# Transposes as 64x64 tiles, variance by ScalarE squares and output in the score banks, in a fused retention and SoLU kernel

## The chip, the cores and the metric

The kernel runs on one core of a Trainium2 chip. The metric is device time in microseconds (us) of one execution; it is about 1.8 us longer than the span that the profile of the same run shows. PE is TensorE, DVE is VectorE, ACT is ScalarE, POOL is GpSimd. Clock means the TensorE clock that the throttle granted, 1 being full speed.

## The reference

Eight batches of eight heads, 576 positions, head size 64, go through decayed linear attention; its output, 4608 tokens of 512, goes through a layer of 1024 with softmax-weighted units, a layer norm and a second matrix.

```python
def _attn_ref(q, k, v):
    scores = scale * np.matmul(q, k.transpose(0, 1, 3, 2))
    ret = scores * Dmat                      # gamma_h ** (i - j), zero above the diagonal
    return np.matmul(ret, v)

def _moe_ref(x, w_in, w_out, g_ln):
    h = x @ w_in                             # 512 -> 1024
    e = np.exp(h - h_max)
    solu = h * e / (np.sum(e) + 1e-09)
    mu, var = mean(solu), mean((solu - mu) ** 2)
    return ((solu - mu) / np.sqrt(var + 1e-06) * g_ln) @ w_out      # 1024 -> 512
```

## The kernel before

The sequence is cut into windows of 256 positions; 36 attention steps (each a half of the heads of one window) feed 36 token tiles of 128, two tiles to a window. In a step PE makes the transposes of query and key (T), the product with the carried state (I), the masked product (V), the new state (K) and the next scores (S). Then come the first-layer product of a tile (h, "first-layer product t"), exp on ACT, the product with h on DVE (solu), the transposes of solu (L) and the second-layer product (o). The layer norm is folded in: the mean comes in as a rank-one correction (for the first 14 tiles on DVE, later through centered weights w2c), and 1/std, called rstd or rs, as the scale of the last copy.

```python
    CAP = dict(... tp=1, qkT=3, s=1, ... xy=1, ... h=1, e=2, oc=2, solu=3, ... lnT=4, o=1, osb=3)
    # PSUM: tp 1 bank, s 2, xy 2, h 2, o 1: all eight

    def qk_tp(i):                     # 8 transposes of 128x128 into the bank tp
        for n, src in enumerate((d["q16"], d["k16"])):
            for hp in range(2):
                for j in range(2):
                    nc.tensor.transpose(out=tp[:, n, hp, j], in_=src[:, j, 2 * hp : 2 * hp + 2, :], identity=ident)
    def qk_ev(i):
        nc.scalar.copy(out=qkT, in_=tp)                       # ACT
    def stats(t):                     # DVE: two bn_stats and a bn_aggr a tile
        ...
    def mm2(t):                       # second-layer product into its own bank o
        ...
    def o_mean(t):                    # DVE, t < 14, reads PSUM, needs no rstd
        nc.vector.scalar_tensor_tensor(out=d["oc"], in0=nws[:, 0], scalar=mean, in1=d["o"], op0=ALU.mult, op1=ALU.add)
    def o_ev(t):                      # ACT
        nc.scalar.activation(out=d["osb"], in_=d["oc"] if t < NE else d["o"], func=ACT.Copy, scale=rs)
```

The order of the first third is a hand-made list for each engine. Before the first second-layer product, dummy matmuls fill PE's holes, in the bank o.

The softmax here doesn't subtract the row's maximum and nothing guards it: scores larger than these inputs give would overflow.

## Time and profile before

225.67 us, the median of three runs. All times are read off the trace as starts of first-layer products (the first of its eight matmuls); "tail" is from product 35 to the end of the span.

| | product 3 starts | 3 to 16 (13 early steps) | 16 to 31 (15 late steps) | 31 to 35 | tail | span |
|---|---|---|---|---|---|---|
| before | 37.04 | 74.93 (5.76 each) | 79.68 (5.31 each) | 19.00 | 14.92 | 225.6 |

### The profile page before, as it was taken

What the parts mean: (1) busy time and instruction counts of PE and PEld (TensorE: products, weight loads), DVE (VectorE), ACT (ScalarE), POOL (GpSimd) and SP (SyncE); (2) the same over time, 40 slices, a digit from 0 to 9 for tenths busy, and PEclk for the clock granted to TensorE, in tenths of its full rate; (3) what the DMA queues carried; (4) which work ended last, traced back from release to release, by engine and by line L of the source; (5) the groups of instructions that cost most, each with busy time, mean ns of one, the idle gap of its engine ahead of it and who ended that gap; (6) DMA issues with size and microseconds to landing.
All of it is one profiled execution on the core that took longest, in us unless ns stands there. A gap on an engine that the chain in (4) does not pass through costs nothing.

```text
span 225.6 us, 7375 instructions
## 1 busy us (share of the span) xinstructions
PE 208.6 (92%) x2983; PEld 122.0 (54%) x2983; DVE 180.0 (80%) x320; ACT 133.2 (59%) x238; POOL 151.6 (67%) x231
## 2 busy tenths in 40 slices
PE   7876989999699999699999999999999999999991
PEld 2423555656355655465665666666566666555440
DVE  6655798999969898999999877778888888876540
ACT  2454776656457876466666566666665556655641
POOL 3439599999959989929669869695968777311010
PEclk9999999999799999999999999999999999999998
DMA  6999999995594600799987777777764552222334
GB/s 178 351 346 346 326 289 289 293 293 135 132 264 109 191 11 3 179 300 310 294 225 202 236 195 205 202 193 193 209 190 107 145 141 53 49 47 60 84 71 117
DMA packets 65635, 42.64 MB, mean 189 GB/s; under 512 B 4024, under 2 KB 59456, under 8 KB 65600
## 3 DMA queue, kind: packets, MB, share of 16 engines
q1 hardware_dynamic: 65200, 41.96, 67.7%
q8 instruction: 23, 0.38, 0.8%
q10 hardware_dynamic: 400, 0.21, 0.6%
q14 instruction: 12, 0.10, 0.2%
HBM read 32.71 MB, written 9.44 MB: 187 GB/s over the span
## 4 chain that ended last, share of the span: by engine, by line
PE 65%; DVE 17%; DMA 5%; POOL 4%; SPq 4%; issue 2%; ACT 1%; DVEq 0%; POOLq 0%; ACTq 0%
PE h_ps L434 22%; PE o_ps L507 21%; PE xy L314 7%; PE tln L483 5%; PE tqk L291 5%; DVE solu L454 4%; PE s_ps L349 4%; DVE bs L460 3%; DVE ret L382 3%; DMA vr<-in_v_dram 3%; SPq L259 3%; DMA masks<-masks 2%; DVE w L471 2%; DVE oc L515 2%; DVE w L468 1%
## 5 line engine op out<-in xcount | busy, mean ns | idle before, releaser
L434 PE MATMUL h_ps<-w_in,xT 128*128 128x512 f16 x288 | 69.7, 386 | 2.0 <-DVE solu L454 1.9
L454 DVE TENSOR_TENSOR solu<-h_ps,e_sb 128x1024 f16<-128x1024 f32 x36 | 43.9, 1219 | 19.2 <-ACT e_sb L447 19.0
L447 ACT ACTIVATE e_sb<-h_ps 128x1024 f32<-128x1024 f32 x36 | 36.8, 1022 | 31.6 <-PE h_ps L434 31.5
L460 DVE BATCH_NORM_STATS2 bs<-solu 128x6 f32<-128x512 f16 x72 | 46.0, 680 | 0.1
L382 DVE TENSOR_TENSOR ret<-s_ps,masks 128x1024 f16<-128x1024 f32 x36 | 43.8, 1215 | 0.2 <-issue 0.2
L434 PEld LDWEIGHTS <-xT 128*128 128x128 f16 x288 | 27.3, 99 | 30.0 <-issue 4.4
L274 POOL TENSOR_TENSOR k<-kr,small 128x512 f16<-128x512 f32 x36 | 37.5, 1041 | 6.9 <-DMA kr<-in_k_dram 5.1
L507 PEld LDWEIGHTS <-lnT 128*128 128x128 f16 x288 | 25.9, 98 | 27.2
L274 POOL TENSOR_TENSOR q<-qr,small 128x512 f16<-128x512 f32 x34 | 35.2, 1039 | 7.0 <-DMA qr<-in_q_dram 6.9
L507 PE MATMUL o_ps<-w2c,lnT 128*128 128x512 f16 x160 | 38.0, 380 | 0.0
L477 POOL TENSOR_TENSOR rs<-w,small 128x2 f32<-128x2 f32 x18 | 12.4, 691 | 30.0 <-DVE w L471 29.9
L299 ACT COPY qkT<-tqk 128x512 f32<-128x512 f32 x36 | 20.9, 580 | 12.6 <-PE tqk L291 12.6
L416 POOL CAST sbd<-g 64x256 f16<-64x256 f32 x64 | 25.6, 400 | 3.3
L507 PE MATMUL o_ps<-w2g,lnT 128*128 128x512 f16 x112 | 26.5, 379 | 0.0
L422 ACT CAST xT<-xy 128x512 f16<-128x512 f32 x36 | 21.4, 593 | 8.1 <-PE xy L314 6.8
L523 ACT ACTIVATE o_sb<-o_ps,rs 128x512 f32<-128x512 f32 x20 | 13.7, 687 | 20.8 <-PE o_ps L507 12.4
L407 POOL TENSOR_TENSOR g<-tt,small 128x128 f32<-128x128 f32 x32 | 13.4, 418 | 16.4 <-DVE tt L403 16.4
L483 PEld LDWEIGHTS <-solu 128*128 128x128 f16 x288 | 18.6, 98 | 9.3 <-DVE solu L454 2.0
L483 PE MATMUL tln<-ident,solu 128*128 128x128 f16 x288 | 22.1, 220 | 1.0 <-DVE solu L454 1.0
L491 ACT COPY lnT<-tln 128x512 f32<-128x512 f32 x36 | 20.8, 579 | 3.5 <-PE tln L483 3.5
L282 POOL CAST v<-vr 128x512 f16<-128x512 f32 x34 | 20.5, 608 | 1.7 <-DMA vr<-in_v_dram 0.3
L314 PE MATMUL xy<-ret,v 64*64 64x128 f16 x576 | 14.6, 219 | 2.0 <-DVE ret L382 2.0
(51 smaller groups left out, 241.7 us busy)
## 6 DMA issues: line engine op xcount, KB each, us to landing
kr<-in_k_dram SPq DMA_DIRECT2D x32, 256.0 KB, 4.9
vr<-in_v_dram SPq DMA_DIRECT2D x32, 256.0 KB, 5.0
qr<-in_q_dram SPq DMA_DIRECT2D x32, 256.0 KB, 4.8
out_dram<-o_sb SPq DMA_DIRECT2D x64, 128.0 KB, 2.4
w_in_f<-in_moe_w_in_dram SPq DMA_DIRECT2D x4, 512.0 KB, 6.8
w_f<-in_moe_w_out_dram SPq DMA_DIRECT2D x4, 512.0 KB, 7.6
qr<-in_q_dram SPq DMA_DIRECT2D x16, 64.0 KB, 2.2
kr<-in_k_dram SPq DMA_DIRECT2D x16, 64.0 KB, 2.7
```

Of the source, the lines that this page charges most:

```text
L274: eng.tensor_tensor(out=t.rearrange("p j h d -> p h j d"), in0=st[i][nm + "r"], in1=g_of(i, base), op=ALU.mult,)
L299: nc.scalar.copy(out=d["qkT"].rearrange("p n h j q -> p (n h j q)").bitcast(FP), in_=d["tp"].rearrange("p n h j q -> p (n h j q)").bitcast ...
L314: nc.tensor.matmul(start=(c, e) not in begun, stop=False, skip_group_check=True, **kw)
L382: nc.vector.tensor_tensor(out=d["ret"].rearrange("p e h j q -> p (e h) (j q)"), in0=d["s"].rearrange("p e h j q -> p (e h) (j q)"), in1=ma ...
L416: nc.gpsimd.tensor_copy(out=s16[ee[e], :, :, ee[e]], in_=st[i]["g"][ee[e]])
L422: nc.scalar.copy(out=d["xT"].rearrange("p c h q -> p c (h q)"), in_=d["av"][:, :, 0:256])
L434: nc.tensor.matmul(out=h_ps[:, hh], lhsT=st[2 * w + dc // 2]["xT"][:, c, dc % 2], rhs=w_in16[:, dc, hh], start=(dc == 0), stop=(dc == 3),)
L447: nc.scalar.activation(out=d["e"], in_=d["h"], func=ACT.Exp, accum_out=ws[w]["se"][:, c : c + 1])
L454: nc.vector.tensor_tensor(out=d["solu"], in0=d["h"], in1=d["e"], op=ALU.mult)
L460: nc.vector.bn_stats(out=bs[:, half], in_=tk[t]["solu"][:, half * 512 : half * 512 + 512])
L483: nc.tensor.transpose(out=tp[:, c], in_=d["solu"][:, c * P : (c + 1) * P], identity=ident)
L507: nc.tensor.matmul(out=d["o"], lhsT=d["lnT"][:, c], rhs=(w2g16 if t < NE else w2c16)[:, c], start=(c == 0), stop=(c == 7))
```

## The change

Its intent: PE is the busiest engine, so the transposes are made four at a time in the four 64x64 quadrants of the array. Two row halves need two banks, so the output loses its bank and goes into the two score banks. DVE is lightened: the variance becomes a square with a sum on ACT, and in exchange DVE evicts the query and key transposes and centers the weights. All engine orders now come out of a greedy simulation with fixed durations; PE's is a fixed pattern after a given head. The dummy matmuls in the holes are gone, but for the first 12.

```diff
-    CAP = dict(raw=5, qk16=3, v16=4, tp=1, qkT=3, s=1, ... lnT=4, o=1, osb=3)
+    CAP = dict(raw=5, qk16=3, v16=4, tl=1, qkT=4, s=1, ... lnT=6, osb=3)      # tl: 2 banks
+    tl = pools["tl"].tile([P, 2, 2, 512], F16, tag="tl", name="tl")
...
+    for r in range(2):                       # row half r -> bank r, column half c -> partitions
+        for c in range(2):
+            x = 64 * (4 * n + 2 * hp + j)
+            turn(tl[ee[c], r, 0, x : x + 64], d[nm][ee[r], j, 2 * hp + c, :], r)
...
-        nc.scalar.copy(out=d["qkT"]..., in_=d["tp"]...)
+        nc.vector.tensor_copy(out=o, in_=i_)
...
-            nc.vector.bn_stats(...)                                             # and bn_aggr
+        nc.scalar.activation(out=d2, in_=tk[t]["solu"], func=ACT.Square, bias=-mean, accum_out=vs)
...
-            d["o"] = pools["o"].tile([P, DM], FP, tag="o", name="o_ps")
+        x = pools["s"].tile([P, 2, 2, 2, P], FP, tag="s", name="o_ps")
+        d["o"] = x[:, 0].rearrange("p h j q -> p (h j q)")
...
-            out=d["oc"], in0=nws[:, 0], scalar=mean, in1=d["o"], ...            # o_mean, before o_ev
+            out=d["osb"], in0=nws[:, 0], scalar=ws[t // 2]["nr"][...], in1=d["osb"], ...   # after o_ev
...
+        x += [f"T{s + 2}", f"L{s - 4}", f"S{s + 1}", f"M1_{s - 2}", f"M2_{s - 4}"]
...
-                    for _ in range(int((start[o.name] - end_pe - 0.3) / 0.36)):
-                        nc.tensor.matmul(out=wm, lhsT=zeros[:, :P], rhs=zeros, start=True, stop=True)
```

The new fixed pattern (the `x +=` line) puts the second-layer product of a tile (M2) two products of the first layer (M1) after its own.

## The prediction

> **What bounds the kernel now.** I read the busy table and the slices first, then the waits of the middle, then the chain of work that ended last, then the groups of the costliest instructions. The busy table and the slices:
>
> ```profile
> PE 208.6 (92%) x2983; PEld 122.0 (54%) x2983; DVE 180.0 (80%) x320; ACT 133.2 (59%) x238; POOL 151.6 (67%) x231
> PE   7876989999699999699999999999999999999991
> DVE  6655798999969898999999877778888888876540
> POOL 3439599999959989929669869695968777311010
> ```
>
> PE is busiest, but only its right half is solid; on the left it has holes while DVE and POOL stand at 9. The window of the second half:
>
> ```profile
> 109.40:205.40 96.00, 96.00 (x1477) 58.90 (x1467) 79.42 (x145) 58.85 (x111) 64.86 (x104) 1.00 0.62 166
> ```
>
> The columns after the length are busy PE, PEld, DVE, ACT, POOL, clock, DMA. PE is busy 96.00 of 96.00 us and no PE wait appears there, so from 109 to 205 us PE is the bound. The chain of work shows what one step (one token tile) consists of:
>
> ```profile
> 112.14 1.73 PE h_ps L434 x8
> 113.87 0.45 PE tln L483 x8
> 114.31 0.11 PE xy L314 x2
> 114.42 0.35 PE s_ps L349 x16
> 114.77 0.35 PE xy L314 x32
> 115.12 1.83 PE o_ps L507 x8
> 116.95 0.45 PE tqk L291 x8
> 117.40 1.73 PE h_ps L434 x8
> ```
>
> A step is 117.40 - 112.14 = 5.26 us (5.37 where the xy product has four matmuls, 5.31 on average). Transposes are 0.90 of it. Before 109 us the steps are longer: the first-layer products number 3 and 16 start at 37.04 and 111.98 us, 5.76 us a step. There the chain is DVE's:
>
> ```profile
> 47.29 1.13 DVE solu L454
> 48.42 1.13 DVE ret L382
> 49.55 0.66 DVE oc L515
> 50.21 1.21 DVE bs L460 x2
> ```
>
> So three phases matter: a fill (to product 3, 37 us), a DVE-limited stretch of 13 steps, a PE-limited rest; the last product (number 35) starts at 210.65 and the kernel ends 14.95 us after it.
>
> **What the Trainium skill says.** (1) "TensorEngine Tiling (Array Packing)", Key Properties: the four 64x64 tiles work independently, and a change of tiling mode drains the engine. The trace agrees: the 64x64 score matmuls start in groups of four 2 to 4 ns apart, with 56 ns to the next group for 128 columns and 28 to 32 ns for the 64 columns of the state product; where the form changes the gap is about 95 ns longer. (2) "PSUM — Partial Sum Buffer", PSUM bank collisions raise a hardware error: two engines must not use one bank's quadrant at once, reads included. In the trace DVE's state read waits for ACT's copy of another part of the same banks:
>
> ```profile
> 88.59 0.29 DVE L398 TENSOR_TENSOR g<-xy,g 128x128 f32<-128x128 f32 x1 [1.04 <-ACT xT L422]
> 92.06 1.19 DVE L471 TENSOR_TENSOR w<-w,mv 128x2 f32<-128x2 f32 x1
> ```
>
> (3) "SBUF — State Buffer", SBUF: two separate sides: a DVE operation with two SBUF inputs and a GpSimd operation exclude each other. The second line agrees: a 128x2 operation, 0.16 us in its median, took 1.19 us beside a GpSimd operation; its group averages 393 ns. (4) "TensorE: Matmul & The Clock Gate", Part 1: an idle array falls to half clock. The kernel before fills its early holes with 18 dummy matmuls; the first 12, on a cold array, averaged 574 ns, the 18 later ones 383 ns.
>
> **The change part by part.**
>
> Transposes. Per step 8+8 transposes of 128x128 become 32+32 of 64x64: 8 groups of four each. At the state product's 30 ns a group that is 0.25 us in place of 0.45, twice: -0.40 us. The number of form changes stays two per step, as the compiled order has all the 64x64 work in one run. PE step: 5.31 - 0.40 = 4.9 us. If PE stayed the bound, 35 steps would give about -14 us.
>
> Variance. The 72 bn_stats (46.0 us) and 36 aggregates (7.5) leave DVE. ACT gets 36 squares; like its exp (1022 + 194 ns) 1.2 us each, 43.8 us. ACT loses the 36 query/key evictions (20.9) and 8 weight scalings (5.8): 133.2 + 43.8 - 26.7 = 150 us. The build still has one table load, so square and exp share a table.
>
> DVE. It gains the 36 evictions (about 0.6 each from the 512 columns, 22 us), 36 tiny negations (4 us) and 8 weight centerings (0.75 plus port stalls, 8 us); 180 - 53.5 - about 5 of aggregate-linked small work + 34 = about 155 us. The mean correction now adds two SBUF tensors in place of one from PSUM, so it can stall on GpSimd; from the 0.1 to 0.2 us mean excess of the small operations I add 0.2 to its 0.74. No engine but PE is near full.
>
> Output in the score banks. This makes a ring. The scores of a step use the pair of banks, the mask reads them, then the second-layer product writes there, ACT evicts it, then the next scores. Around the ring in the compiled order, with durations of the trace: second product's first matmul to its eviction's start 1.99 (120.31 to 122.30); eviction to ACT's next copy, xT, 0.59; xT to the state read of DVE, which by (2) waits for it, 0.65; state read and its successor 0.54; mask 1.22 + 0.05; then the next second product. Sum 5.03 us. That is longer than PE's 4.9, so it is the ring and not PE that sets the later steps: a gain of 0.28, not 0.40. In the early steps DVE carries mean correction, eviction, product, mask and state: 1.16 + 0.2 + 0.64 + 1.13 + 0.67 + 0.2 + 0.54 + some 0.5 of small ones = 5.0, so the ring or DVE gives 5.1, plus 0.7 for each weight centering.
>
> Fill. The compiled POOL order puts the second state cast behind four loads' work (q2, k2, v2, q3). In the kernel before, q2's work starts at 16.58 us; its q and k scalings take 1.0 and v casts 0.58. So this cast ends at 16.58 + 3 x 1.0 + 0.6 + 0.8 = 21.0, where before the product waiting for it ran at 14.05. First-layer product 0 then starts at about 22.5 instead of 15.28, on a cold array (no dummy matmuls any more), +1.7. The second weight matrix is queued behind step 4's loads: by the positions in the queue and the landings seen before (5.37 MB at 20.5 us, 7.47 MB at 26.25) its last piece lands at 28.4 instead of 26.25. Walking the orders: product 1 at 30.5 (held by DVE's mask, eviction and product), state cast 3 at 35.1, product 2 at 36.6, the weight column sum 38.8 to 40.5, its two ACT copies until 43, only then scores 5 (same banks), mask until 45.5 behind a weight centering, second product 0 until 47.3, product 3 at 48.8. Before: 37.04. The fill loses 11.8 us.
>
> Sum: 48.8 + 11 early steps x 5.12 + 2 without a state product x 4.8 + 4 remaining centerings x 0.7 = 117.5 for product 16 (before 111.98). Fifteen ring steps x 5.05: 193.2. Four shorter last steps, bounded by product-exp-product (4.35 seen at the end before, 4.4 now): 210.9 for product 35. Tail: two second products remain with one output buffer, but the kernel before had four left; by the same durations it comes to 14.9. End: 225.8 us.
>
> **Rivals.** (a) PE stays the bound, the designer's intent: the ring's state read may run before xT in several steps (in the compiled order of some early steps it does), steps of 4.9, and the fill loses only 8 us as loads overlap better. Then 45 + 28 x 4.9 + 17.7 + 14.9 = 215 us. For it: the orders were made by a simulation that aims at 5.0; a change of this size was made to be kept. Against it: in all late steps the state read waits for ACT. (b) Stalls: port stalls of DVE's new two-SBUF-input work, a cold array in the fill, POOL held in turn; 5.3 a step and product 3 at 51 give 51 + 28 x 5.3 + 17.7 + 14.9 = 232. For it: single stalls of over 1 us exist before. Against it: POOL's work falls by the 10.1 us of centering. (c) 64x64 transposes do not run four abreast; then the step stays at 5.3 and the time is that of (b). The state product's groups speak against it. (d) ACT the bound: 4.1 to 4.3 us a step, not likely.
>
> **Range and chances.** The working gives 225.8. I take 224.5, a little to the side of (a), as the list walk sums many waits that may overlap. Rivals (a) and (b) are 215 and 232; I call 217 to 231 the 80% range. Faster by over 2% needs less than 221.2: 0.33. Slower needs more than 230.2: 0.17. Within: 0.50.
>
> **What would show it.** Right if: transposes take 0.25 us per 32; the late steps are 5.0 to 5.1 with PE idle 0.1 to 0.2 a step before the second product, waiting for DVE's mask; product 3 starts at 46 to 51 us; first product 0 after 21 us at half clock; DVE busy about 155, ACT 150. Wrong if: PE has no waits after 60 us and steps of 4.9 (then (a)), if product 3 starts before 44 us, or if the transposes take 0.4 and more.

## More of the kernel before

The two fences here are not in the prediction. The first is PE's clock in 40 slices (tenths of full speed), the second two products of the fill (start, length, engine, line, operation, tiles):

```profile
PEclk9999999999799999999999999999999999999998
```

```profile
23.88 1.89 PE L434 MATMUL h_ps<-w_in,xT 128*128 128x512 f16 x8
...
33.29 1.89 PE L507 MATMUL o_ps<-w2g,lnT 128*128 128x512 f16 x8
```

The clock row stands at 9 from the start, and already first-layer product 1, at 23.88 us, takes 1.89 us (1.82 to the next instruction's start), like second-layer product 0 at 33.29.

Before, for the first 14 tiles, the output's bank came free when the mean correction had read it, which needs no rstd; later it was the ScalarE copy, which does, but no scores stood behind that bank.

## The result, and the profile after

The changed kernel took 242.33 us (237.74 to 242.53, four runs), against 226.32 of the kernel before in the same rounds: slower by a ratio of 1.058 (95% interval 1.043 to 1.073). Ratios are the mean time of one kernel's fast runs over that of the other's of the same rounds, so they are not quite the ratio of the medians. Executions over 1.5% slower than the fastest of the same kernel are left out of the means. Two of six executions counted, and one of these, the profiled one, was the quickest seen. The other four counted as slow only beside it: the control below, the same kernel on another occasion, gave that same level throughout, 241.57 us (240.42 to 242.51), and 1.069. I compare experiments with that control. Both profiles, by the same starts:

| | product 3 | 3 to 16 | 16 to 31 | 31 to 35 | tail | span |
|---|---|---|---|---|---|---|
| predicted | 48.8 | 68.7 | 75.7 | 17.7 | 14.9 | 225.8 |
| changed, first profile | 49.61 | 76.19 | 77.86 | 18.06 | 14.24 | 236.0 |
| changed, control | 52.27 | 76.45 | 78.37 | 18.06 | 14.24 | 239.4 |

Against the kernel before, the control lost 15.2 us in the fill and 1.5 in the early steps, and won 1.3, 0.9 and 0.7 in the three later parts. Against the prediction it is 13.6 us too long: 3.5 in the fill, 7.7 in the early steps, 2.7 in the late ones. The busy table and slices of the first profile:

```profile
PE 199.0 (84%) x4693; PEld 110.9 (47%) x4693; DVE 174.1 (74%) x335; ACT 154.2 (65%) x266; POOL 147.9 (63%) x223
...
PE   7324469499898869898999899999999999999962
...
DVE  6670897978898997899889786868778687663220
...
PEclk9855999799999979999999999999999999999999
```

PE has become less busy, and its left half is no fuller than before. DVE was to fall from 180 to about 155 and stands at 174. The clock row has 8, 5, 5 where it had 9. The waits of the same profile between 50 and 110 us (total us, times, longest):

```profile
ACT o_sb L497 <- POOL rs L477: 8.0, 4, 2.0
...
PE s_ps L343 <- ACT o_sb L497: 5.1, 4, 2.2
```

The output copy waits for rstd, and the next scores wait for that copy. The prediction's ring has the second wait and not the first. Here is one instance in the control, line by line (start, length; DVE, POOL, ACT and PE in turn):

```profile
60.40 0.97 DVE L468 SCALAR_TENSOR_TENSOR w<-se 128x2 f32<-128x2 f32 x1
...
66.28 1.50 DVE L506 SCALAR_TENSOR_TENSOR o_sb<-nws,nr,o_sb 128x512 f32<-128x512 f32 x1
...
60.31 1.03 POOL L255 TENSOR_TENSOR q<-qr,small 128x512 f16<-128x512 f32 x1
...
61.72 0.70 POOL L477 TENSOR_TENSOR rs<-w,small 128x2 f32<-128x2 f32 x1 [0.37 <-DVE w L469]
...
66.19 1.03 POOL L255 TENSOR_TENSOR q<-qr,small 128x512 f16<-128x512 f32 x1
...
62.45 0.69 ACT L497 ACTIVATE o_sb<-o_ps,rs 128x512 f32<-128x512 f32 x1 [2.00 <-POOL rs L477]
...
63.19 0.42 PE L343 MATMUL s_ps<-qkT 64*64 64x128 f16 x16 [0.89 <-ACT o_sb L497]
```

Two things are to be seen. First a chain: DVE's floor of the variance (w, 60.40), GpSimd's power (rs, 61.72), the copy (62.45), the scores (63.19). ACT stood 2 us, PE 0.89. This comes with a window's first tile, because rstd is made for two tiles together and has to wait for the second one: the first six steps are 5.06, 6.21, 5.44, 6.23, 6.06, 7.75. The chain itself has not become slower: in windows 8 to 13 the power ends 8.7 to 8.9 us after the start of the window's second first-layer product, where it took 8.4 to 8.5 in the kernel before. What moved is the copy. From tile 4 to tile 29 the second-layer product started 18.6 to 21.5 us after the first-layer product of its tile; from tile 3 to tile 29 it now starts 11.8 to 17.1 after it. In the kernel before the copy of tile 18 found its rstd 7.25 us old:

```profile
135.62 0.69 POOL L477 TENSOR_TENSOR rs<-w,small 128x2 f32<-128x2 f32 x1 [0.82 <-DVE w L471]
...
143.56 0.69 ACT L523 ACTIVATE o_sb<-o_ps,rs 128x512 f32<-128x512 f32 x1 [1.06 <-issue]
```

In the control the copy of the first tile of each window from 1 to 13 starts 0.03 to 0.06 us after rstd is there. Second, DVE's small instructions are stretched. The floor is 128x2 and took 0.97 us beside a GpSimd scaling that ran from 60.31 to 61.34; the mean correction took 1.50 us beside the next one. The Trainium skill, "SBUF — State Buffer", SBUF: two separate sides, says just this, that a DVE instruction with two SBUF inputs and a GpSimd instruction that reads SBUF hold a port pair in turn for their whole length; the trace agrees. The correction's mean length went from 740 ns (one operand in PSUM) to 1074.

### The profile page after: what moved, and what is told of

Its sections match the earlier page's. It is cut to its first block, busy times and chain, and to the rows that moved or that the text cites.

```text
span 236.0 us, 10927 instructions
## 1 busy us (share of the span) xinstructions
PE 199.0 (84%) x4693; PEld 110.9 (47%) x4693; DVE 174.1 (74%) x335; ACT 154.2 (65%) x266; POOL 147.9 (63%) x223
## 5 line engine op out<-in xcount | busy, mean ns | idle before, releaser
L448 DVE SCALAR_TENSOR_TENSOR solu<-h_ps,e_sb 128x1024 f16<-128x1024 f32 x36 | 44.0, 1221 | 19.1 <-ACT e_sb L441 18.9
L441 ACT ACTIVATE e_sb<-h_ps 128x1024 f32<-128x1024 f32 x36 | 36.9, 1024 | 17.7 <-PE h_ps L428 17.3
L497 ACT ACTIVATE o_sb<-o_ps,rs 128x512 f32<-128x512 f32 x36 | 24.7, 687 | 34.9 <-POOL rs L477 16.5
L460 ACT ACTIVATE d<-solu,nm 128x1024 f16<-128x1024 f16 x36 | 41.5, 1153 | 2.7 <-DVE nm L452 2.4
L490 PE MATMUL o_ps<-w2c,lnT 128*128 128x512 f16 x176 | 41.6, 379 | 1.9 <-ACT lnT L483 1.9
L263 POOL CAST v<-vr 128x512 f16<-128x512 f32 x34 | 23.7, 698 | 3.4 <-PE xy L308 1.9
L298 DVE COPY qkT<-tl 128x512 f32<-128x512 f32 x36 | 24.5, 681 | 0.5 <-PE tl L269 0.3
L343 PE MATMUL s_ps<-qkT 64*64 64x128 f16 x576 | 15.6, 224 | 11.0 <-ACT o_sb L497 7.0
L483 ACT COPY lnT<-tl 128x512 f32<-128x512 f32 x36 | 21.1, 586 | 1.3 <-DVE qkT L298 0.7
L308 PE MATMUL xy<-qkT,sbd 128*128 128x128 f16 (+1 forms) x128 | 12.6, 215 | 10.5 <-POOL sbd L410 9.4
L308 PEld LDWEIGHTS <-sbd 128*128 128x128 f16 x128 | 9.4, 99 | 19.0 <-POOL sbd L410 10.0
```

The costliest lines, as they stand in the source:

```text
L263: copy(out=t, in_=st[i]["vr"])
L298: nc.vector.tensor_copy(out=o, in_=i_)
L308: nc.tensor.matmul(start=(c, e) not in begun, stop=False, skip_group_check=True, **kw)
L441: nc.scalar.activation(out=d["e"], in_=d["h"], func=ACT.Exp, accum_out=ws[w]["se"][:, c : c + 1])
L448: nc.vector.scalar_tensor_tensor(out=d["solu"], in0=d["h"], scalar=1.0, in1=d["e"], op0=ALU.mult, op1=ALU.mult, accum_out=x["ss"][:, c : c ...
L460: nc.scalar.activation(out=d2, in_=tk[t]["solu"], func=ACT.Square, bias=x["nm"][:, c : c + 1], accum_out=x["vs"][:, c : c + 1])
```

## The experiments

Each kernel is the changed one with the edit shown, and was timed in rounds with the kernel before. The first number is the median of all four runs, the second the ratio to the kernel before over fast runs alone; one run of fillwm, warm2 and warm2b and two of bnback counted as slow. "Output right" means that the result passes the comparison. Two give wrong results (norscale and noodrs); one, nood, leaves out a small term and still passes the comparison, but isn't a right kernel either.

### again: the control

> The changed kernel itself, unchanged, as the control of this chip. It should give the same two levels as before: 236 to 238 us with a mean clock near 0.956, and 241 to 242.5 us near 0.93. First-layer product 3 starts near 49.6 us, product 16 near 125.8, product 31 near 203.7 if the profile falls in the faster level. If the profile falls in the slower one, its windows should show in which stage the other 4 to 5 us lie.

241.57 us, ratio 1.0687 (1.061 to 1.077); all four runs between 240.4 and 242.5. The two levels that I expected are not there as such: the first profile's run was the better end. In the control's profile the extra time lies in the fill (product 1 at 30.79 against 29.44, product 2 at 38.72 against 36.03), the later parts are the same to 0.5 us each.

### norscale: the copy needs no rstd

```diff
-        nc.scalar.activation(out=d["osb"], in_=d["o"], func=ACT.Copy, scale=ws[t // 2]["rs"][:, t % 2 : t % 2 + 1])
+        nc.scalar.activation(out=d["osb"], in_=d["o"], func=ACT.Copy, scale=1.0)
```

> The output eviction of ScalarE scales by 1 in place of rstd (a wrong result on purpose), so the score banks come free without waiting for the variance chain (square, floor, GpSimd's power). Theory A, the early steps are long because the eviction waits for rstd: the alternation 5.1/6.2 goes, 13 early steps shrink from 76.2 to 67 to 70 us, the whole by 6 to 9 us. Theory B, the early steps are long because VectorE is full (mean correction, centering, port stalls): under 2 us of gain. Theory C, a cold array in the fill: no gain.

237.61 us, 1.052. The early steps fell only from 76.45 to 73.98 us: the strict pattern of 5.1 and 6.2 went, but steps of 5.1 to 6.8 came in its place. So theory A alone is not the cause; the gain is between the two theories.

### rstile: rstd for each tile

```diff
-            op(f"fl{w}", "DVE", "xx", [f"sp{t - 1}", f"sp{t}"], ...)      # if c: once a window
-            op(f"rs{w}", "POOL", "rs", [f"fl{w}"], ...)
+        op(f"fl{t}", "DVE", "xx", [f"sp{t}"], ...)
+        op(f"rs{t}", "POOL", "rs", [f"fl{t}"], ...)
```

> The floor and rstd are made for each tile in place of each window of two tiles (18 more floor pairs on VectorE, 18 more powers of 0.69 us on GpSimd), result right. An even tile's eviction then needs only its own square, a step earlier. Theory A: the early steps lose most of the waits of the eviction for rstd, 4 to 7 us faster than the changed kernel. Theory B: more VectorE work, so 0 to 3 us slower. Theory C: no change.

238.11 us, 1.052, output right: 3.5 us, just short of theory A. The early steps took 75.78, nearly as before; 1.6 us of the gain is in the late ones (76.76), which now have 5.12 us each. The wait for rstd is gone: from tile 3 on rstd is ready at least 3.0 us before the copy. In the early steps the profile still puts 7.7 us of the copy's waits down to GpSimd (L263), but that is a false name, as here: the instruction named had ended at 66.67 and rstd at 62.99, and the copy starts 0.09 us after the second-layer product ends (65.47 + 1.89 = 67.36):

```profile
65.47 1.89 PE L490 MATMUL o_ps<-w2g,lnT 128*128 128x512 f16 x8
...
67.45 0.69 ACT L497 ACTIVATE o_sb<-o_ps,rs 128x512 f32<-128x512 f32 x1 [0.79 <-POOL v L263]
```

So without the wait for rstd, but with more small work on DVE (70.5 us busy in these steps against 68.9), the early steps gain almost nothing.

### warm: dummy matmuls, placed badly

```diff
+            n = dict(I1=20, S5=4, M2_0=7).get(o.names[0], 0)
+            if n:
+                wm = pools["h"].tile([P, DFF], FP, tag="h", name="wm")
+            for _ in range(n):
+                nc.tensor.matmul(out=wm[:, 0:512], lhsT=zeros[:, :P], rhs=zeros, start=True, stop=True)
```

> Dummy matmuls keep the array busy in the fill: 20 before the second inter-window product (idle 13.3 to 20.8 us), 4 before scores 5 and 7 before the second-layer product 0. Theory C, the cold array and its clock cost time and split the runs in two levels: product 0 takes 1.7 to 1.9 in place of 3.05 us, the second-layer product 0 likewise in place of 3.36, together 2.5 to 3 us, and the slower level of 242 us is no longer seen. Theories A and B: at most 3 us, and the early steps stay at 5.86.

241.11 us, 1.066: no difference from the control. It was no test, though. The dummies write to the first-layer banks, whose former content (the transposed gains) DVE copied out only at 17.9 us. The 20 of them started there and took 6.9 us, 0.35 each; product 0 started at 25.24. The idea is tested again in warm2 below.

### nood: DVE's mean corrections left out

```diff
-        nc.vector.scalar_tensor_tensor(out=d["osb"], in0=nws[:, 0], scalar=nr, in1=d["osb"], op0=ALU.mult, op1=ALU.add)
...
-        nc.vector.tensor_tensor(out=d["nr"], in0=d["nm"], in1=d["rs"], op=ALU.mult)
```

> VectorE's early mean corrections (14 of about 1.07 us) and their scalars (7 of about 0.4 us) are left out, all else in the same order (a wrong result on purpose). Theory B, VectorE is full in the early steps with work that the prediction put at 5.0 us a step and that takes 5.65: removing about 1.3 us a step makes the 13 early steps drop from 76.4 to 66 to 71 us (then the ring or PE sets 5.1 and the waits for rstd stay), the whole by 6 to 10 us against the unchanged kernel's 241.6. Theory A, the wait for rstd sets them: the alternation of 5.1 and 6.2 us stays and the gain is under 3 us.

234.69 us, 1.034. The early steps fell from 76.45 to 70.29, the larger half of what the prediction missed. What is left alternates between 5.13 and 5.6, and in it the copy still waits for rstd. So DVE's load is the larger cause and the wait for rstd the smaller. (In this profile product 3 came at 54.10, 1.8 us later than in the control, as first-layer product 2 ran cold too, 3.43 us; the 70.29 is counted from there.)

### odps: the early output path as before the change

```diff
-            out=d["osb"], in0=nws[:, 0], scalar=ws[t // 2]["nr"][...], in1=d["osb"],
+            out=d["oc"], in0=nws[:, 0], scalar=ws[t // 2]["nm"][...], in1=d["o"],       # before the copy
...
-           lambda t=t: mm2(t), [("s", [f"oe{t}"])], wide=True)
+           lambda t=t: mm2(t), [("s", [f"od{t}" if t < NE else f"oe{t}"])], wide=True)
```

> The early output path as in the kernel before: VectorE corrects the mean straight from the score bank, so only one operand lies in SBUF and no scalar with rstd is needed; ScalarE scales from SBUF later. Result right. Theory B with port stalls: the correction falls from 1.07 to about 0.75 us, the 0.4 us scalars go, and the eviction no longer waits for rstd; early steps 69 to 73 us in place of 76.4, the whole 3 to 7 us faster. If the corrections' place in VectorE's order matters more (the scores now wait for VectorE, which is busy), no gain or up to 3 us of loss.

237.27 us, 1.048, output right. The early steps took 74.23, 2.2 less than the control: short of the range. They became quite regular, eight of thirteen at 5.62 us, and the trace shows why. The correction is now in the score banks' ring and DVE makes it after solu. So solu starts at 113.04, the correction at 114.38, the scores at 115.17 (0.50 us waited for it), the product at 115.52, its exp after it, then the next solu at 118.66: one loop through three engines (DVE, PE, ACT), which no single engine's load shows.

### fillpool: the first state casts ahead of later loads

```diff
-            op(f"sm{i}", "POOL", "st_b", [f"sd{i}"], at(i - 1, 2.2), ...)
+            op(f"sm{i}", "POOL", "st_b", [f"sd{i}"], at(i - 1, 2.2) - (10 if i < 4 else 0), ...)   # and so for sc
```

> In the fill GpSimd makes the first four state products and casts ahead of the query and key scalings of later steps. By the prediction's step on the fill, first-layer product 0 was late because the second state cast stood behind four loads' work: it should start near 15 to 17 us in place of 21.7 to 22.2. If the fill is a chain through that cast, product 3 starts 4 to 6 us earlier than 52 and so does the end; if what comes later (weights, score banks, cold array) sets product 3, it starts within 2 us of where it did.

236.27 us, 1.042, output right. Product 0 started at 16.74, as expected, 5.4 us earlier. Product 3 started only 2.8 us earlier, at 49.51, between the two expectations; the whole gained 5.3 us by the medians. The cast was late as the prediction's walk had it, but half of its lateness was hidden behind what comes after. The first profile of the unchanged kernel also had product 3 at 49.61, so 2 to 3 us here are not much more than the scatter of the fill between profiles.

### fillwm: the weight column sum in the first-layer banks

```diff
-        t = pools["s"].tile(...)[:, 0]...                  # HEAD "... M1_2 T5 WM"
+        t = pools["h"].tile([P, DFF], FP, tag="h", name="w_sum")[:, 0:512]     # after S5
```

> The weight column sum goes to the first-layer banks after scores 5, in place of the score banks before them. By the prediction's step on the fill, scores 5 wait for its two ScalarE copies and second-layer product 0 waits on the mask after them: from product 2 to product 3 takes 13.55 us and should fall to 9 to 11, the end 3 to 4 us earlier. If the second-layer weights' landing sets that stretch, it stays at 13.

243.44 us, 1.069: no gain. From product 2 to product 3 took 14.9 us, not 9 to 11. Scores 5 ran at 41.88 in place of 45.18, but the sum now waited 3.26 us for solu of tile 2, which holds the first-layer banks, and the second-layer product 0 started at 48.95 in place of 47.43. The sum also ran cold (3.60 us in place of 1.90). One bank's wait was traded for another's, so the run neither confirms nor refutes that the score banks set this stretch.

### noodrs: both early suspects away

The edits of nood and norscale together.

> Both suspects of the early steps are taken away at once, in the same order of work: no mean corrections and no scalars for them on VectorE, and the eviction scales by 1, so it waits for no rstd (a wrong result on purpose). So far the first alone gained 6.2 us in the 13 early steps (76.4 to 70.3), the second alone 2.5. If the two together are the whole of what the prediction missed (it had 68.7 us for these steps, with mean corrections), the steps fall to the ring's 5.03 to 5.15 each, 66 to 68 us, with no alternation left. If a third cause holds them, they stay at 70.

231.55 us, 1.024. The early steps took 69.04 us, 7.4 less than the control, a little above the 66 to 68 expected: most steps are 5.0 to 5.1, one is 6.53 (four weight centerings lie near there), a few 5.5. The prediction had 68.7 for these steps. So the wait for rstd and DVE's correction work with its stalls together account for the early miss. But the run takes the corrections away whole (14 us less DVE work in these steps), not only what they cost beyond the prediction. The windows from 60 to 109 us, of the control and of this run (busy PE, PEld, DVE, ACT, POOL, then clock, DMA, GB/s):

```profile
60.00:109.00 49.00, 42.49 (x1046) 24.13 (x1045) 44.29 (x80) 31.97 (x56) 35.12 (x52) 0.97 0.62 165
```

```profile
60.00:109.00 49.00, 46.38 (x1166) 26.50 (x1165) 40.90 (x76) 35.24 (x64) 40.09 (x59) 1.00 0.70 197
```

In the control DVE is the busiest of the five, in this run PE.

### tp128: 128x128 transposes in the changed kernel

```diff
-            turn(tl[ee[c], r, 0, x : x + 64], d[nm][ee[r], j, 2 * hp + c, :], r)     # 32 of 64x64
+            nc.tensor.transpose(out=tl[:, n, 0, x : x + P], in_=d[nm][:, j, 2 * hp : 2 * hp + 2, :], identity=ident)
...                                      # solu's likewise; T and L are 0.45 in the simulation's durations
```

> The transposes of the changed kernel are again of 128x128 (8 and 8 a step, 0.45 us each group, one quadrant at a time), all else kept but the simulated order that follows. My reading of the changed kernel: early steps are not PE's, so they change by under 2 us; the late steps are PE's and the ring's at 5.02 to 5.15 us, and PE's own work goes to 5.3 to 5.4, so the 15 late steps take 79.5 to 82 in place of 78.4 and the last four 19 in place of 18.1: 2 to 5 us slower in all. If the tiles did not run four abreast or did not matter, no change.

249.93 us, 1.105, output right: 8.4 us of the medians slower than the control (1.105 against 1.069), more than the 2 to 5 expected. The early steps stayed (76.98), the late ones took 83.54, 5.57 each in place of 5.22; 2.4 us of the loss lie in the fill (product 3 at 54.62). PE was busy for 83.4 of the 83.54 us. A late step of the control and the same part of tp128:

```profile
173.31 1.89 PE L490 MATMUL o_ps<-w2c,lnT 128*128 128x512 f16 x8
175.03 0.28 PE L308 MATMUL xy<-qkT,sbd 128*128 128x128 f16 x2
...
175.61 0.30 PE L269 MATMUL tl<-ident,q 64*64 64x64 f16 x16
175.74 0.31 PE L269 MATMUL tl<-ident,k 64*64 64x64 f16 x16
175.86 0.49 PE L269 MATMUL tl<-ident,solu 64*64 64x64 f16 x32
176.17 0.41 PE L343 MATMUL s_ps<-qkT 64*64 64x128 f16 x16
```

```profile
163.85 0.40 PE L277 MATMUL tl<-ident,q 128*128 128x128 f16 x4
164.08 0.39 PE L277 MATMUL tl<-ident,k 128*128 128x128 f16 x4
164.30 0.61 PE L282 MATMUL tl<-ident,solu 128*128 128x128 f16 x8
164.84 0.42 PE L339 MATMUL s_ps<-qkT 64*64 64x128 f16 x16
```

Counted from start to start, the transposes take 176.17 - 175.61 = 0.56 us as 64x64 tiles and 164.84 - 163.85 = 0.99 as 128x128; the state product before them, which the larger form has to wait for, gives another 0.1. The step grew from some 5.1 us (where nothing else waits) to 5.57, nearly as much. So in the late steps PE is the bound, and the 64x64 tiles are worth what PE saves there.

### bnback: variance on DVE, query and key evictions on ACT

```diff
-        nc.scalar.activation(out=d2, in_=tk[t]["solu"], func=ACT.Square, bias=..., accum_out=...)
+        for half in range(2):
+            nc.vector.bn_stats(out=bs[:, half], in_=tk[t]["solu"][:, half * 512 : half * 512 + 512])
+        nc.vector.bn_aggr(out=x["mv"][:, c], in_=bs)
...
-        nc.vector.tensor_copy(out=o, in_=i_)        # qk_ev
+        nc.scalar.copy(out=o, in_=i_)
```

> The exchange between VectorE and ScalarE is undone in the changed kernel: variance by VectorE's statistics again (1.3 us and an aggregate a tile), query and key evictions on ScalarE again. VectorE gains about 0.75 us a step. If VectorE is what the early steps wait for, they take 83 to 88 us in place of 76.4; the late steps, where VectorE has 5 us of room in 20, change by under 2 us. Whole: 7 to 13 us slower. If VectorE is not the limit, under 3 us, or even a gain, as the variance is then a ScalarE square and a queue shorter.

253.16 us, 1.110, output right (its two fast runs took 250.67 and 251.43). The early steps took 84.76 us, within the range for a full DVE; but DVE was busy for only 74.7 of them (68.9 of 76.45 in the control), so waits grew with its work. The late ones took 83.74, which I had not expected: they alternate between 5.06 and 5.84, and ACT's copy waits for rstd 16 times in the run, 22.4 us in all. With the variance in DVE's queue rstd comes later, and the score banks wait for it there too. So the exchange of work is worth 4% inside the changed kernel, and the new ring makes a late rstd dear everywhere. The new durations also changed the simulated order of the fill: the second state cast came at 14.07 in place of 20.31 and product 3 at 47.67, which hides 4.6 us of the loss.

### ne4: a right version from these findings

```diff
-NE = 14
+NE = 4                                              # 4 mean corrections; with rstile and fillpool
...
-  op(f"wp{x}", "DVE", "wp", [f"lwo{c}", "gc", "nw1"], at(6 + x * 0.75, 4.0), ...)
+  op(f"wp{x}", "DVE", "wp", [f"lwo{c}", "gc", "nw1"], at(5 + x * 0.4, 2.0), ...)
```

> A right version from what the runs showed: weight centering on VectorE as early as it can be, so that only 4 in place of 14 tiles need a mean correction; floor and rstd for each tile; GpSimd's first four state casts ahead of later loads. If VectorE's corrections and the wait for rstd are the early loss and the state cast a part of the fill's: product 3 at 49 to 51, the 13 early steps 66 to 70, 16 to 31 as in the run with rstd for each tile (76.8), the whole 224 to 230 us, that is 11 to 17 faster than the changed kernel and about level with the kernel before.

232.75 us, 1.029, output right, just above the range. From product 7 on the early steps are 5.0 to 5.5, but the four steps after product 3 took 27.8 us, because the centerings moved there.

### warm2: a warm array in the fill

```diff
-    op("gc", "DVE", "gc", ["G"], at(3, 0.0), ...)
+    op("gc", "DVE", "gc", ["G"], at(-2, 0.0), ...)       # the gains' copy early: it holds the banks
...
+            n = {'S0': 7, 'I0': 4, 'I1': 31, 'S5': 5, 'M2_0': 7}.get(o.names[0], 0)      # and 42 before M1_1
+            for _ in range(n):
+                nc.tensor.matmul(out=..., lhsT=zeros[:, :P], rhs=zeros, start=True, stop=True)
```

> The first warm run was no test: its dummies stood behind a copy of the gains that VectorE made only at 17.9 us, and ran cold. Here that copy is early and dummies fill the holes from the start: 17 before the first transpose, 7, 4 and 31 before scores 0 and the inter-window products 0 and 1, 42 small ones before first-layer product 1, 5 and 7 before scores 5 and second-layer product 0. If the missing dummies (which the change took out) are a part of the fill's loss: the granted clock of the slices up to 50 us is 0.9 to 1, the products of 3.2 to 3.6 us take 1.9, product 3 starts 3 to 6 us before 52, the end likewise, and the run-to-run spread of 236 to 242 us narrows. If VectorE and GpSimd set the fill, product 3 moves by under 1.5 us.

Three runs took 238.0 to 240.6 us at clocks of 0.98 (ratio 1.056); the profiled one took 711.62. It says nothing of the kernel: the matmuls ran at about a quarter of full speed. The group of the first-layer products in this run (busy us, mean ns, idle before; in the control 73.2 and 400):

```profile
L428 PE MATMUL h_ps<-w_in,xT 128*128 128x512 f16 x288 | 239.1, 1077 | 0.0
```

From one product's start to the next operation's start it took 6.3 to 6.6 us for eight matmuls there, some 0.8 each, against 0.22 between most matmuls of the control.

### ne4warm: both together

The edits of ne4 and of warm2, with 11 dummies in place of 31 before inter-window product 1, as that hole is shorter here.

> The right version of before (early centering, 4 corrections, rstd for each tile, early state casts) with the array kept busy in the fill in the same way. If both add up: product 3 at 44 to 47 in place of 49.3, the whole 3 to 5 us under 232.75, 227 to 230, still not under the kernel before. If the fill there is set by VectorE's centering, no gain over 1.5 us.

231.59 us, 1.023, output right. Product 3 came at 44.62, as expected, but the step after it took 9.83 us, and the end moved by only 1.2 us. DVE and PE in that step:

```profile
45.53 1.83 DVE L562 SCALAR_TENSOR_TENSOR w2c<-w_f,gln,nws 128x512 f16<-128x512 f32 x2
...
49.68 2.55 PE L490 MATMUL o_ps<-w2g,lnT 128*128 128x512 f16 x8 [3.16 <-ACT e_sb L441]
```

DVE put two centerings ahead of the state read, which came only at 47.28; ACT's copies and exp stood behind that read, and DVE's mask, which second-layer product 1 must await too, ended at 49.6. The line names the exp; both came last at nearly the same time. What a warm PE saved, DVE's order took back.

### warm2b: the profile that was missing

> The same kernel as warm2 once more, as its profile fell in one run of 710 us (its three other runs took 238.0 to 240.6 at a clock of 0.98). Expected: a median of 238 to 241, the clock row at 9 up to 50 us, the first-layer products 0 and 1 and second-layer product 0 at 1.9 us in place of 3.2 to 3.6. If the cold array is worth its 4 to 5 us of longer products, product 3 starts at 47 to 49; if other engines set the fill, at 50 to 52.

238.66 us, 1.049, output right. Products of the fill in the control and here, then the clock row of this run:

```profile
30.79 3.56 PE L428 MATMUL h_ps<-w_in,xT 128*128 128x512 f16 x8 [2.65 <-DVE solu L448]
...
47.43 3.20 PE L490 MATMUL o_ps<-w2g,lnT 128*128 128x512 f16 x8 [1.83 <-DVE ret L376]
```

```profile
30.57 1.89 PE L428 MATMUL h_ps<-w_in,xT 128*128 128x512 f16 x8
...
36.82 3.38 PE L428 MATMUL h_ps<-w_in,xT 128*128 128x512 f16 x8
...
47.03 1.89 PE L490 MATMUL o_ps<-w2g,lnT 128*128 128x512 f16 x8 [0.21 <-DVE ret L376]
```

```profile
PEclk9999797999999998999999999999999999999999
```

The cold products are back at 1.89 (one, at 36.82, isn't), product 3 starts at 50.24, 2.0 us earlier, and the ratio is 2.0 points lower. What the cold array is worth is not sharp: 2.0 us at product 3, 2.9 by the medians, some 4.5 by the ratio, whose interval (1.037 to 1.061) just touches the control's (1.061 to 1.077); warm2's ratio of 1.056 is 2.8 us. The scatter of the fill is of this size too. So 2 to 4.5 us; at product 3 less than the 4 to 5 of the longer products. Product 3 is at the edge of the second expectation, that other engines set the fill.

### n8warm and n8head: last tries

n8warm has 8 corrections and centerings spread from step 7 on; n8head besides puts product 3 ahead of scores 5, brings the first transposes of solu forward and leaves out the 12 dummies before scores 5 and second-layer product 0. Both have the other edits of ne4warm.

```diff
+NE = 8
+  op(f"wp{x}", "DVE", "wp", [f"lwo{c}", "gc", "nw1"], at(7 + x * 0.5, 0), ...)
+        if s == 4:                                                  # n8head
+            x = "WM I4 V4 K5 T6 M1_3 S5 M2_0".split()
```

> As ne4warm, but with 8 corrections and the weight centering spread over steps 7 to 11, as in ne4warm two centerings ahead of a state read cost the step after product 3 nearly 5 us (9.83 us long). Product 3 at 44 to 45 again, that step 5 to 6.5, the whole 224 to 228, 4 to 7 under ne4warm's 231.6 and about level with the kernel before. If VectorE takes the time back later, under 2 us.

231.24 us, 1.017, output right: no more than ne4warm within the intervals. Product 3 came at 46.06 and the step after it took 7.33, both longer than expected.

> As n8warm, with first-layer product 3 ahead of scores 5 in PE's order, where the array stood idle for two waits. Product 3 at 37 to 40; the end within 1.5 us of n8warm's if the score banks' ring (weight sum, scores 5, second product 0) sets this stretch, 2 to 4 us earlier if PE's own order did.

230.26 us, 1.016 (1.008 to 1.024). Product 3 started at 37.37, as early as in the kernel before, and product 4 at 53.73, where n8warm has 53.40. So PE's order was not what set this stretch. In this trace second-layer product 1 waited 3.54 us, until 47.77, for DVE's mask, which stood behind a floor of 0.90 us, a scalar, a weight centering of 1.16 and the state reads; then it ran cold, 3.57 us. This is the best right version; its ratio lies 1.6% above the kernel before, by less than the 2% at which a verdict is given (it is "unclear", as for noodrs, ne4warm and n8warm). No run beat the kernel before.

## Why the prediction was wrong

It said 224.5 us, 217 to 231, and slower with a chance of 0.17. By its own steps:

**Transposes: right, a little mis-sized.** The query and key transposes took 0.25 us as it said, those of solu 0.31. The two together fell by 0.33 us (0.89 to 0.56), not 0.40. In the late step of 5.02 us, attention's four products took 0.93 us where they had taken 0.81, most of it at the inter-window product (0.21 for 0.11); that gave 0.12 back. The step shortened by 0.24, so PE's own step is 5.02 to 5.1, not 4.9. The ring's terms, by the way, add up to 5.04 and not 5.03.

**"It is the ring and not PE that sets the later steps": the number stood, the mechanism fell.** Late steps free of other waits are 5.08 to 5.12 us on average (15 of them took 76.16 to 76.76 in n8warm, noodrs and rstile) where it said 5.05. But PE has no idle time left there, and tp128 lengthened the step by nearly the whole of what it added to PE. Rival (a), PE as the bound, was right for this part, only at 5.1 and not 4.9; that the ring's 5.05 came so near was luck. The late stretch also had 2 us more of single stalls: one step of 6.23 with a wait for rstd, one of 6.08 in which PE stood 0.84 us for nothing that the profile shows.

**Early steps, "the ring or DVE gives 5.1": this is the step that failed.** Its sum for DVE was right. The instructions of the control's 13 early steps, each counted to the next one's start, add up to about 66 us without the four centerings, 5.1 a step against 5.0. With the centerings DVE was busy for 68.9 us, about the 68.7 that the prediction gave the whole stretch; but the stretch took 76.45 (5.88 a step), as DVE also stood idle for 8.0. The prediction gave it no idle time, though the kernel before had 5.7 us of it there (busy 69.2 of 74.93).

Two things were missing. The ring had no term for rstd. "Second product's first matmul to its eviction's start 1.99" was read at tile 14, whose copy does need rstd, but in an order where rstd had been there for 6.3 us; with the second-layer product moved a step or more forward it was not, and the chain square, floor, power, copy, scores became part of the ring. And the two bounds were joined as a maximum. DVE stands inside the ring (state read, mask, floor), so a full DVE makes rstd and the masks late, and late scores leave DVE idle. The runs size it: 2.5 us for rstd alone (norscale), 6.2 for the corrections alone (nood), 7.4 for both (noodrs), of a miss of 7.7. How much each wait inside the loop takes is not shown: with rstd early by 3 us (rstile) the early steps kept 75.8, so rstd is the smaller part. No run put the second-layer product back by a step, which would test the order itself.

**DVE at 155 us: wrong by 19.** Both kernels' tables give the terms. The corrections grew by 4.6 us in all (10.4 to 15.0, 1.07 each), which the sum had left out. It took off 5 us of small work, but the floor's two instructions cost 11.6 us before and after. It did not list the reads of the accumulators (3.0) and the corrections' scalars (2.7). The evictions took 24.5 in place of 22, the negations 5.5 in place of 4. The stretching by GpSimd, for which 0.2 us was put on a correction, is in some of these: in the control the 13 first instructions of the floor that overlapped GpSimd work averaged 0.59 us, the other five 0.15.

**Fill: right in size, partly in cause.** 48.8 us for product 3, 49.6 and 52.3 measured. Its walk was right from step to step, some 2 us early: column sum at 38.8 (40.91 in the control), its copies until 43 (45.1), then scores 5 (45.18), the mask behind a centering until 45.5 (47.4), then second product 0 (47.43). It counted one cold product, +1.7; the control had three of 3.2 to 3.6 us, and warm2b gained 2.0 there. The late state cast is real but worth 2.8 in place of the larger part I gave it. The column sum in the score banks was named as a cause; fillwm, which moved it, gained nothing, though it met another wait. With the cast and most of the cold array mended (n8warm), or the cast and PE's order (n8head), product 4 still starts at 53.4 to 53.7, against 57.33 in the control and 42.84 before. I would argue that the chain of scores, column sum and second products through the same two banks sets it, with DVE's mask in it; n8head's wait of 3.54 us for the mask and its cold product fit that. But no run takes the chain away: what makes up these 10 us stays open.

**Rivals.** (b), 5.3 a step with product 3 at 51, was nearest, and its reasons (port stalls, a cold array, POOL held) all occurred. Its 232 was still short: it gave the early steps 5.3 us, and had no wait for rstd either. (c) and (d) did not happen.

## What to carry to other kernels

When a buffer changes hands, ask what the instruction that frees it now waits for: here the bank was the same size and the copy the same length, but the next scores had come to depend on a chain through three engines, and a new order had used up the 5 to 12 us by which rstd was mostly early before. Where an engine near its limit also stands in a ring, don't take the larger of the two times; its queue delays the ring and the ring idles it, so leave room for that idle time, and remove both at once to see what they cost together. And a part that works where it is the bound (here the transposes, 5.6 us from product 16 to 35 by tp128) can be lost, and more, in a stretch whose order was rewritten along with it, so time the stretches separately.

## What the Trainium skill lacked or had wrong

- "TensorEngine Tiling (Array Packing)", Key Properties, has that tiles of 64x64 run in parallel, but no time for transposes in them: 16 and 16 of the 64x64 transposes took 0.25 us and 32 of solu 0.31, against 0.45 and 0.54 in tp128 for the same data in 128x128.
- "TensorE: Matmul & The Clock Gate", Part 1, gives when the clock falls, and a share of the span for the ramp at the start, but not what a fill with holes is worth to a kernel: here three products were longer by 1.3 to 1.7 us each, and mending them (while another one came out cold) brought 2 to 4.5 us of 241.6.
- The same page mentions a clock stuck at a quarter for 50 us and more; one run here stayed there for its whole 710 us (some 0.8 us for a matmul of 512 columns against 0.22), and the profile listed a granted clock of 1.0 for it.
- "SBUF — State Buffer", SBUF: two separate sides, has the lock between DVE and GpSimd right; no page says what it costs an instruction this small: a 128x2 instruction of 0.15 us took 0.97 beside a GpSimd scaling of 1.03.
